# Batch 0's start shared with GpSimd and cut by head pairs, and batch 1's v behind the first pieces of w_out

## Chip, cores and metric

The kernel runs on one core of one Trainium2 chip. The metric is device time in microseconds (us), where lower is better. Engines are named as the profile names them: PE is TensorE (matmuls; PEld its weight loads), DVE is VectorE, ACT is ScalarE, POOL is GpSimd, and SP is the sync engine, which here only issues DMAs.

## What is computed

Linear attention is followed by a two-layer network with a leaky ReLU. Sizes: 8 batches, 8 heads, 576 positions, head size 64; 4608 tokens of width 512; hidden width 2048. All inputs and the output are f32 in HBM.

```python
q_s = softmax(q, axis=-1)              # over the 64 of a head
k_s = softmax(k, axis=2)               # over the 576 positions
kv  = einsum('bhsd,bhse->bhde', k_s, v)
x   = einsum('bhsd,bhde->bhse', q_s, kv) -> (4608, 512), heads side by side
h   = x @ w_in                         # 512 x 2048
out = maximum(0.01 * h, h) @ w_out     # 2048 x 512
```

## The kernel before

**Layout.** A batch of q, k or v is loaded as a tile of 128 partitions x 4 x 9 x 64: 4 "head rows" (`HL`), 9 rows of positions (`R`), and each partition half holds another head. Two head rows side by side make a head pair (`gg` is 0 or 1). After attention x is kept transposed in `xT`, four blocks of 128 channels by 4608 tokens; block `2*hh + gg` belongs to pair `gg`, so that blocks 0 and 2 come from the first pair and blocks 1 and 3 from the second. `layer1` takes the blocks in the order 0, 2, 1, 3.

**Tiles.** The network runs over 9 tiles of 512 tokens. In a tile, layer 1 makes 16 slices `j` of 128 hidden channels (4 matmuls each, then `leaky` on ACT), and layer 2 sums over the 16 slices into four 128 x 512 outputs. Tile 0 is special: its layer 1 is cut into two halves of 256 tokens, and its layer 2 runs with `j` outermost, so that the weights are needed one slice after the other. The other tiles wait for all of layer 1.

**Order.** The order of the instructions is written by hand: each engine takes its own in program order. Attention of later batches is hooked into the loops of the network: `at(t, u, ...)` files functions for tile `t` and step `u`, and `run(t, u)` calls them. In tile 0, u of 0 to 15 are the slices of the first half of layer 1, 16 to 31 those of the second half, 32 to 47 those of layer 2. Batch 1 must be done by the end of tile 0: its k and q work stands on DVE, POOL and ACT from u = 15, its kv at u = 38 (line 586), its transposes at 41 to 46, its `attend` at 47 (line 592).

**Batch 0's start (lines 507 to 557).** `q_first` (L228) takes DVE's maxima and 16 small exponentials on ACT, whose sums are collected as they run. k's maximum over the positions goes over DVE (`k_tree`, L149) and PE (`k_max_pe`, `k_all_pe`); it is subtracted from PSUM (`k_sub_ps`, L352) and ACT takes the exponential. ACT then casts v to bf16 (`v_cast`, L209), DVE normalises q's first four rows as a whole (`q_norm`, L277), PE transposes them, ACT and DVE keep the transposes, `kv_pair` (L360) and `kd_one` make the normalised kv of a pair, and `attend` (L408) makes a block of x. Layer 1 of the first 256 tokens begins with blocks 0 and 2 for j of 0 to 7 (`begun`, line 643), and takes blocks 1 and 3 afterwards. q's rows 4 and 5 (`R1`) and 6 to 8 (`R2`) follow at u = 3 and 5 and are transposed at u = 11 and 13. `wake` (L322) is a run of matmuls on zeros.

**The loads.** SP issues the plain loads (queue q1), POOL the weight loads, which cast f32 to bf16 on the way (queue q0). Both run on the same 16 DMA engines. w_in comes in two halves by hidden channels (`load_w_in`, L129), each in four pieces: two for pair 0's blocks (`gg` 0), two for pair 1's. POOL issues the first half after `gate` (line 509), a copy of one element of the second pair of batch 0's k; the second after line 534, a copy of an element that DVE's last subtraction writes. `hold_sync` (L503) makes SP wait: it issues a tiny DMA that reads the last columns of a weight piece, so whatever SP issues behind it goes out only when that piece has landed. Hold 0 (line 560) reads block 0 of w_in's second half, which its first piece brings; behind it stand batch 1's k (two pieces), q and v. POOL issues w_out in five pieces (slices 0-1, 2-3, 4-7, 8-11, 12-15; line 565) when batch 1's first k piece has landed (line 564). Hold 1 waits for w_out's fourth piece, then SP loads batch 2.

**Buffers.** PSUM has six shared banks (`psB`), taken in turn by all small products, and two for outputs.

Of the kernel before, what the change touches and what calls it, by code (L numbers as in the profile page):

```python
# [8 lines left out]
FP32 = mybir.dt.float32  # L9
BF16 = mybir.dt.bfloat16  # L10
# [9 lines left out]
L = 64  # L20
R = 9
# [4 lines left out]
def kernel(  # L26
# [122 lines left out]
    def k_tree(b, hs, steps=slice(0, 4)):  # L149
        n = hs.stop - hs.start  # L150
        ks = st[b]["k"][:, hs]
        if steps.start == 0:
            st[b]["t4"] = mx_pool.tile([P, HL, 4, D], FP32, name="t4")[:, 0:n]
        t4 = st[b]["t4"]
        t2, t1 = t4[:, :, 0:2], t4[:, :, 0]
        for o, i0, i1 in (
            (t4, ks[:, :, 0:4], ks[:, :, 4:8]),
            (t2, t2, t4[:, :, 2:4]),
            (t1, t1, t4[:, :, 1]),
            (st[b]["kmax"][:, hs], t1, ks[:, :, 8]),  # L160
        )[steps]:
            nc.vector.tensor_tensor(out=o, in0=i0, in1=i1, op=ALU.max)  # L162
# [65 lines left out]
    def q_first(b, rs):  # L228

        n = rs.stop - rs.start  # L230
        nmax = small_pool.tile([P, HL, n], FP32, name="nmax")
        qsum = small_pool.tile([P, n, HL], FP32, name="qsum")
        for hs in (slice(0, 2), slice(2, 4)):
# [3 lines left out]
            for h in range(hs.start, hs.stop):  # L237
                for r in range(n):
                    nc.scalar.activation(
                        out=st[b]["qe"][:, rs.start + r, h],  # L240
                        in_=st[b]["q"][:, h, rs.start + r],
                        func=AF.Exp,
                        bias=nmax[:, h, r : r + 1],
                        accum_out=qsum[:, r, h : h + 1],
                    )
        st[b]["qsum"] = qsum

    def q_first_rec(b, rs):
        n = rs.stop - rs.start
        st[b]["qrec", rs.start] = qrec = small_pool.tile([P, n, HL], FP32, name="qrec")  # L250
        nc.vector.reciprocal(out=qrec, in_=st[b]["qsum"])

    def q_sub(eng, b, rs):
        n = rs.stop - rs.start
# [146 lines left out]
    def q_keep(eng, b, r0, n, gs=slice(0, 4)):  # L401
        o, i = st[b]["qT"][:, gs, r0 : r0 + n], st[b]["ps", r0][:, gs]
        if eng is nc.scalar:
            eng.copy(out=o, in_=i)
        else:
            eng.tensor_copy(out=o, in_=i)
# [91 lines left out]
        st[b]["q"] = load(q, b, "q_raw", whole)  # L498
        st[b]["v"] = load(v, b, "v_raw", whole)

    held = const_pool.tile([1, 2, 128], BF16)

    def hold_sync(i, src):  # L503
        nc.sync.dma_start(out=held[:, i], in_=src)
# [45 lines left out]
    kd_rec(0, 1, 0)  # L550
    kd_rec(0, 1, 1)
    kd_one(nc.vector, 0, 1, 0)
    kd_one(nc.vector, 0, 1, 1)
    q_max(0, R1)
    q_sub(nc.gpsimd, 0, R1)
    q_max(0, R2)
    q_sub(nc.gpsimd, 0, R2)
# [12 lines left out]

    at(0, 3, lambda: q_exp(0, R1), lambda: q_sum(0, R1), lambda: q_norm(0, R1))
    at(0, 5, lambda: q_exp(0, R2), lambda: q_sum(0, R2), lambda: q_norm(0, R2))
    at(0, 11, lambda: q_transpose(0, 4, 2), lambda: q_keep(nc.vector, 0, 4, 2))
    at(0, 13, lambda: q_transpose(0, 6, 3), lambda: q_keep(nc.vector, 0, 6, 3))
    at(0, 15, lambda: attend(0, [0, 2], 256, 256, nc.scalar))
    at(0, 15, lambda: attend(0, [1, 3], 256, 256, nc.vector))
    at(0, 17, lambda: attend(0, [0, 1, 2, 3], 512, 64, nc.scalar))
    at(0, 15, lambda: k_begin(1), lambda: q_begin(1), lambda: k_tree(1, H0), lambda: k_tree(1, H1))
    at(0, 15, lambda: k_allmax(1), lambda: k_sub(nc.gpsimd, 1, H0), lambda: k_sub(nc.vector, 1, H1))
    at(0, 15, lambda: q_max(1, RA), lambda: q_sub(nc.gpsimd, 1, RA))  # L580
    at(0, 15, lambda: q_max(1, RB), lambda: q_sub(nc.gpsimd, 1, RB))
    at(0, 29, lambda: k_exp(1, H1))
    at(0, 31, lambda: k_exp(1, H0), lambda: v_cast(nc.scalar, 1, 0))
    at(0, 33, lambda: q_exp(1, RA), lambda: q_sum(1, RA), lambda: q_norm(1, RA))
    at(0, 33, lambda: v_cast(nc.scalar, 1, 1), lambda: q_exp(1, RB))
    at(0, 38, lambda: kv(1), lambda: kd_make(1), lambda: q_sum(1, RB), lambda: q_norm(1, RB))
    at(0, 41, lambda: q_transpose(1, 0, 2), lambda: q_keep(nc.scalar, 1, 0, 2))
    at(0, 42, lambda: q_transpose(1, 2, 2), lambda: q_keep(nc.scalar, 1, 2, 2))
    at(0, 45, lambda: q_transpose(1, 4, 3), lambda: q_keep(nc.scalar, 1, 4, 3))
    at(0, 46, lambda: q_transpose(1, 7, 2), lambda: q_keep(nc.scalar, 1, 7, 2))  # L590
    for i in range(8):
# [48 lines left out]
        return [g_pool.tile([P, 2, TT], BF16, name="gj") for _ in range(NF // 2)]  # L640

    g_sb = g_tiles()
    begun = []
    for j in range(0, 8, 2):
        ph = psB_pool.tile([P, 2, 256], FP32, name="ph", tag=BANK_TAG)
        for i in range(2):
            layer1(j + i, ph[:, i], 0, 256, slice(0, 2), i == 0)
        begun.append(ph)
    attend(0, [1, 3], 0, 256, nc.scalar)
    for half in range(2):  # L650
        for j in range(0, NF, 2):
            part = slice(2, 4) if begun else slice(0, 4)
            ph = begun.pop(0) if begun else psB_pool.tile([P, 2, 256], FP32, name="ph", tag=BANK_TAG)
            for i in range(2):
                layer1(j + i, ph[:, i], 256 * half, 256, part, i == 0, i == 1)
                if i == 1:
                    leaky(g_sb[j // 2][:, :, 256 * half : 256 * half + 256], ph)
                run(0, 16 * half + j + i)
# [66 lines left out]
```

## Time and profile before

| what | us |
|---|---|
| three runs | 295.09 (median), 294.68, 296.09 |
| span of the profiled execution (first to last instruction) | 293.0 |
| the profiled execution's own time | not given; the median lies 2.1 above the span |
| PE busy | 278.8 (95%) |
| ACT, DVE, POOL busy | 150.8, 144.9, 85.6 |
| PE idle before layer 1's matmuls (L452) | 4.3 |
| batch 1's attends begin on PE | 52.48 |
| granted TensorE clock, mean | 0.998 |

The timeline view has one row for a stretch of like instructions: start, duration, line, operation, tiles, shape, count, and in brackets the idle time ahead of it and what ended it. The windows view has, for each stretch, its length, the busy time of PE, PEld, DVE, ACT and POOL with the number of instructions, then the granted clock, the mean busy share of the 16 DMA engines (over 1 where transfers overlap on an engine) and the GB/s that they moved; bytes of a casting load count as bf16. The view of DMA issues gives size and time from issue to landing. A busy PE isn't a PE at its peak, since the ends of matmuls are modelled.

### The profile page before, as it was taken

The page shows a single profiled execution, that of the slowest core. Times are in us where ns is not written, and L with a number is a line of the kernel's source. Part 1 is how long each engine was busy: PE and PEld are TensorE (multiplying, and loading weights), DVE is VectorE, ACT ScalarE, POOL GpSimd, SP SyncE. Part 2 cuts the span into 40 slices and gives each one's busy share as a digit, 9 for nine tenths or more (in the row PEclk, how much of TensorE's full clock was granted, in tenths as well). Part 3 has the DMA queues.
Part 4 walks back from the last instruction along what each step waited for, and adds up shares of the span by engine and source line. Part 5 has one row for each costly group of instructions (what it writes and reads, how often), then busy time and mean ns, then how long its engine had stood idle before and what let it go on. Part 6 is the DMA issues. An engine that isn't in the chain of part 4 may idle for free.

```text
span 293.0 us, 4255 instructions
## 1 busy us (share of the span) xinstructions
PE 278.8 (95%) x1634; PEld 139.1 (47%) x1661; DVE 144.9 (49%) x240; ACT 150.8 (51%) x272; POOL 85.6 (29%) x61
## 2 busy tenths in 40 slices
PE   6596999999999999999999999999999999999995
PEld 2265845444544455454445544544455444444443
DVE  3947957885491597189367455735440200110011
ACT  4956682777058605951695338532854066007500
POOL 4645280025029307802920292029300000000000
PEclk9999999999999999999999999999999999999999
DMA  7999999694729553874399138923141310131032
GB/s 258 307 211 387 247 191 400 160 345 152 135 55 326 196 116 91 273 266 88 70 326 276 36 72 289 294 55 72 38 81 38 72 36 1 38 72 36 0 72 73
DMA packets 36580, 45.76 MB, mean 156 GB/s; under 512 B 15952, under 2 KB 19280, under 8 KB 36560
## 3 DMA queue, kind: packets, MB, share of 16 engines
q1 hardware_dynamic: 33120, 41.16, 47.4%
q0 software_dynamic: 3280, 4.20, 8.2%
q8 instruction: 13, 0.21, 0.3%
q10 hardware_dynamic: 160, 0.13, 0.1%
q14 instruction: 7, 0.06, 0.1%
HBM read 36.70 MB, written 9.44 MB: 157 GB/s over the span
## 4 chain that ended last, share of the span: by engine, by line
PE 84%; DMA 3%; DVE 3%; ACT 2%; POOL 2%; issue 1%; POOLq 0%; ACTq 0%
PE pout L473 40%; PE ph L452 39%; DMA w_in_sb<-in_moe_w_in_dram 3%; PE pkv L295 3%; PE po L440 2%; POOL k_raw L195 1%; DVE t L162 1%; ACT vb L213 1%; DVE k_raw L356 1%; ACT xT L422 1%; PE psum_qt L389 1%; POOL w_in_sb L133 0%; ACT qe L264 0%; DVE xT L424 0%; DVE m L179 0%
## 5 line engine op out<-in xcount | busy, mean ns | idle before, releaser
L452 PE MATMUL ph<-xT,w_in_sb 128*128 128x512 bf16 (+1 forms) x626 | 127.1, 357 | 4.3 <-DMA w_in_sb<-in_moe_w_in_dram 1.9
L473 PE MATMUL pout<-w_out_sb,gj 128*128 128x512 bf16 (+2 forms) x580 | 129.1, 373 | 0.9 <-issue 0.5
L461 ACT ACTIVATE gj<-ph 128x512 bf16<-128x512 f32 x144 | 82.5, 604 | 58.5 <-PE ph L452 57.9
L452 PEld LDWEIGHTS <-w_in_sb 128*128 128x128 bf16 x640 | 62.0, 98 | 66.1 <-issue 5.5
L473 PEld LDWEIGHTS <-gj 128*128 128x128 bf16 x592 | 56.9, 98 | 61.6
L467 DVE COPY out_sb<-pout 128x512 f32<-128x512 f32 (+1 forms) x34 | 22.7, 675 | 90.7 <-PE pout L473 82.1
L195 POOL TENSOR_TENSOR k_raw<-k_raw,kall 128x2304 f32<-128x2304 f32 (+1 forms) x6 | 29.1, 4844 | 86.2 <-DVE kall L187 55.8
L273 DVE TENSOR_REDUCE qsum<-qe 128x36 f32<-128x2304 bf16 (+4 forms) x11 | 19.8, 1800 | 39.5 <-ACT qe L264 39.5
L256 POOL TENSOR_TENSOR q_raw<-q_raw,qmax 128x2304 f32<-128x2304 f32 (+4 forms) x11 | 31.1, 2839 | 23.5 <-DVE qmax L226 23.5
L446 ACT CAST xT<-po 128x320 bf16<-128x320 f32 (+1 forms) x48 | 16.8, 402 | 40.0 <-PE po L440 40.0
L203 ACT ACTIVATE ke<-k_raw 128x2304 bf16<-128x2304 f32 (+2 forms) x11 | 17.5, 1595 | 9.7 <-POOL k_raw L195 9.4
L280 DVE TENSOR_TENSOR qe<-qe,qrec 128x2304 bf16<-128x2304 bf16 (+4 forms) x12 | 21.1, 1758 | 0.4
L226 DVE TENSOR_REDUCE qmax<-q_raw 128x36 f32<-128x2304 f32 (+4 forms) x11 | 19.4, 1788 | 0.0
L264 ACT ACTIVATE qe<-q_raw 128x2304 bf16<-128x2304 f32 (+4 forms) x11 | 16.9, 1535 | 0.0
L215 POOL CAST vb<-v_raw 128x1152 bf16<-128x1152 f32 x12 | 13.4, 1151 | 0.0
L467 ACT COPY out_sb<-pout 128x512 f32<-128x512 f32 (+1 forms) x3 | 1.6, 549 | 17.5 <-PE pout L473 17.5
L162 DVE TENSOR_TENSOR t<-k_raw 128x1024 f32<-128x1024 f32 (+1 forms) x10 | 10.1, 1010 | 0.4 <-DMA k_raw<-in_k_dram 0.2
L324 PE MATMUL pout<-zero 128*128 128x512 bf16 x26 | 8.9, 469 | 1.4 <-POOL zero L101 1.3
L162 DVE TENSOR_TENSOR t<-t 128x256 f32<-128x256 f32 (+2 forms) x20 | 9.6, 478 | 0.7
L440 PE MATMUL po<-qX,kd 128*128 128x320 bf16 (+1 forms) x48 | 9.8, 286 | 0.1
L295 PEld LDWEIGHTS <-ke 64*128 64x128 bf16 x252 | 7.2, 93 | 3.2 <-ACT gj L461 1.7
L295 PE MATMUL pkv<-vb,ke 64*128 64x129 bf16 x252 | 8.5, 216 | 0.1
(55 smaller groups left out, 103.5 us busy)
## 6 DMA issues: line engine op xcount, KB each, us to landing
out_dram<-out_sb SPq DMA_DIRECT2D x70, 128.0 KB, 2.4
q_raw<-in_q_dram SPq DMA_DIRECT2D x7, 1152.0 KB, 8.2
v_raw<-in_v_dram SPq DMA_DIRECT2D x7, 1152.0 KB, 11.0
k_raw<-in_k_dram SPq DMA_DIRECT2D x6, 1152.0 KB, 5.8
k_raw<-in_k_dram SPq DMA_DIRECT2D x4, 576.0 KB, 5.6
w_in_sb<-in_moe_w_in_dram POOLq DMA_DIRECT2D x8, 256.0 KB, 7.4
w_out_sb<-in_moe_w_out_dram POOLq DMA_DIRECT2D x3, 512.0 KB, 12.2
v_raw<-in_v_dram SPq DMA_DIRECT2D x2, 576.0 KB, 7.4
```

The lines of the kernel that those rows point to most:

```text
L162: nc.vector.tensor_tensor(out=o, in0=i0, in1=i1, op=ALU.max)
L195: eng.tensor_tensor(out=ks, in0=ks, in1=st[b]["kall"][:, hs].unsqueeze(2).to_broadcast([P, n, R, D]), op=ALU.subtract,)
L203: nc.scalar.activation(out=st[b]["ke"][:, :, hs].rearrange("p r h d -> p h r d"), in_=st[b]["k"][:, hs], func=AF.Exp,)
L226: nc.vector.tensor_reduce(out=m, in_=st[b]["q"][:, :, rs], axis=AX.X, op=ALU.max)
L256: eng.tensor_tensor(out=qs, in0=qs, in1=st[b]["qmax", rs.start].unsqueeze(3).to_broadcast([P, HL, n, D]), op=ALU.subtract,)
L273: nc.vector.reduce_sum(out=qsum, in_=st[b]["qe"][:, rs], axis=AX.X)
L280: nc.vector.tensor_tensor(out=qes, in0=qes, in1=st[b]["qrec", rs.start].unsqueeze(3).to_broadcast([P, n, HL, D]), op=ALU.mult,)
L295: nc.tensor.matmul(pkv[hh][:, gg, 0:129], lhsT=st[b]["ke"][rows, r, 2 * gg : 2 * gg + 2].rearrange("p h d -> p (h d)"), rhs=vb2[b % 2][row ...
L452: nc.tensor.matmul(ph, lhsT=w_in_sb[:, cb, j * P : (j + 1) * P], rhs=xT[:, cb, c0 : c0 + n], start=(i == 0 and first), stop=(i == NB - 1 a ...
L461: nc.scalar.activation(out=o, in_=ph, func=AF.Prelu, alpha=LEAKY_SLOPE)
L467: copy(out=out_sb, in_=pout)
L473: nc.tensor.matmul(pout, lhsT=g_sb[j // 2][:, j % 2, tsub * P : (tsub + 1) * P], rhs=w_out_sb[:, j, os], start=(j == 0), stop=(j == NF - 1),)
```

## The change

In batch 0, POOL opens w_in's first half on the first k pair. POOL then casts v's pairs to bf16 and multiplies q's first four rows by their reciprocal sums, a pair at a time, and issues w_in's second half behind that. PE transposes q by pairs, each pair's kv, kd and x blocks are made apart, and layer 1 is begun block by block in two groups of slices, with the other pair's attends and the transposes of rows 4 to 7 between. q's late rows go in pairs (4-5, 6-7) and row 8 alone. Two `wake` calls (4 and 3 matmuls on zeros) become one of 2. Hold 0 reads block 1 of w_in's second half, which its third piece brings. A new hold 2 on w_out's second piece stands ahead of batch 1's v. In batch 1 ACT's two casts of v stand behind the first q exponential, and hooks move.

```diff
-    R1, R2 = slice(4, 6), slice(6, R)
+    R1, R2, R3 = slice(4, 6), slice(6, 8), slice(8, R)
@@ q_first: the same work, its sums kept by pair
+    def q_first_rec(b, gg):
+        st[b]["qrec2", gg] = qrec = small_pool.tile([P, RA.stop, 2], FP32, name="qrec2")
+        nc.vector.reciprocal(out=qrec, in_=st[b]["qsum", gg])
+
+    def q_first_norm(eng, b, gg):
+        qes = st[b]["qe"][:, RA, 2 * gg : 2 * gg + 2]
+        eng.tensor_tensor(
+            out=qes,
+            in0=qes,
+            in1=st[b]["qrec2", gg].unsqueeze(3).to_broadcast([P, RA.stop, 2, D]),
+            op=ALU.mult,
+        )
+
+    def q_turn_first(b, gg):
+        n = RA.stop
+        ps = psB_pool.tile([P, 2, n, L], BF16, name="psum_q2", tag=BANK_TAG)
+        for r in range(n):
+            nc.tensor.matmul(
+                ps[:, :, r],
+                lhsT=st[b]["qe"][:, r, 2 * gg : 2 * gg + 2].rearrange("p h d -> p (h d)"),
+                rhs=ident,
+                is_transpose=True,
+                start=(r == 0),
+                stop=(r == n - 1),
+            )
+        st[b]["ps2", gg] = ps
+
+    def q_keep_first(eng, b, gg):
+        o, i = st[b]["qT"][:, gg::2, RA], st[b]["ps2", gg]
...
@@ batch 0
-    nc.gpsimd.tensor_copy(out=gate[:, 0:1], in_=st[0]["k"][:, HL - 1, R - 1, D - 1 : D])
+    nc.gpsimd.tensor_copy(out=gate[:, 0:1], in_=st[0]["k"][:, 1, R - 1, D - 1 : D])
     load_w_in(0)
...
     wake(2)
+    q_first_rec(0, 0)
+    v_cast(nc.gpsimd, 0, 0)
+    q_first_norm(nc.gpsimd, 0, 0)
     k_tree(0, H1, slice(1, 4))
...
     k_exp(0, slice(1, 2))
-    v_cast(nc.scalar, 0, 0)
-    v_cast(nc.scalar, 0, 1)
+    q_first_rec(0, 1)
+    v_cast(nc.gpsimd, 0, 1)
+    q_first_norm(nc.gpsimd, 0, 1)
+    load_w_in(1)
     k_sub_ps(0, 1)
-    nc.gpsimd.tensor_copy(out=gate[:, 0:1], in_=st[0]["k"][:, HL - 1, R - 1, D - 1 : D])
-    load_w_in(1)
+    q_turn_first(0, 0)
+    q_keep_first(nc.scalar, 0, 0)
     k_exp(0, H1)
-    q_first_rec(0, RA)
-    q_norm(0, RA)
     kv_pair(0, 0)
-    wake(4)
-    q_transpose(0, 0, 4)
-    kv_pair(0, 1)
+    wake(2)
     for hh in range(2):
         kd_rec(0, 0, hh)
         kd_one(nc.vector, 0, 0, hh)
-    q_keep(nc.scalar, 0, 0, 4, slice(0, 4, 2))
-    q_keep(nc.vector, 0, 0, 4, slice(1, 4, 2))
-    attend(0, [0, 2], 0, 256, nc.scalar)
-    wake(3)
+    attend(0, [0], 0, 256, nc.vector)
+    attend(0, [2], 0, 256, nc.scalar)
+    q_turn_first(0, 1)
+    q_keep_first(nc.vector, 0, 1)
+    kv_pair(0, 1)
...
-    hold_sync(0, w_in_sb[0:1, 0, F - 128 : F])
+    hold_sync(0, w_in_sb[0:1, 1, F - 128 : F])
     st[1]["k"] = load(k, 1, "k_raw", [(H0, ALLR), (H1, ALLR)])
     st[1]["q"] = load(q, 1, "q_raw", [(ALLH, ALLR)])
-    st[1]["v"] = load(v, 1, "v_raw", [(ALLH, ALLR)])
     nc.gpsimd.tensor_copy(out=gate[:, 0:1], in_=st[1]["k"][:, 0, 0, 0:1])
     for j0, j1 in ((0, 2), (2, 4), (4, 8), (8, 12), (12, 16)):
         load_w_out(slice(j0, j1))
+    hold_sync(2, w_out_sb[0:1, 3, 0:128])
+    st[1]["v"] = load(v, 1, "v_raw", [(ALLH, ALLR)])
     hold_sync(1, w_out_sb[0:1, 11, 0:128])
     load_all(2)
@@ hooks of tile 0: q_rest is q_exp, q_sum, q_norm
+    at(0, 0, lambda: q_rest(R1))
+    at(0, 3, lambda: q_rest(R2))
+    at(0, 12, lambda: q_rest(R3))
+    at(0, 13, lambda: attend(0, [0, 2], 256, 256, nc.scalar))
+    at(0, 13, lambda: attend(0, [1, 3], 256, 256, nc.vector))
+    at(0, 17, lambda: q_transpose(0, 8, 1), lambda: q_keep(nc.scalar, 0, 8, 1))
+    at(0, 21, lambda: attend(0, [0, 1, 2, 3], 512, 64, nc.scalar))
...
+    at(0, 31, lambda: k_exp(1, H1))
+    at(0, 33, lambda: k_exp(1, H0))
+    at(0, 36, lambda: q_exp(1, RA), lambda: q_sum(1, RA), lambda: q_norm(1, RA))
+    at(0, 36, lambda: v_cast(nc.scalar, 1, 0), lambda: v_cast(nc.scalar, 1, 1), lambda: q_exp(1, RB))
+    at(0, 36, lambda: q_sum(1, RB), lambda: q_norm(1, RB))
+    at(0, 42, lambda: kv(1), lambda: kd_make(1))
@@ layer 1 of tile 0's first 256 tokens
+    def begin(js, parts):
+        phs = [psB_pool.tile([P, 2, 256], FP32, name="ph", tag=BANK_TAG) for _ in js]
+        for i, between in parts:
+            for j, ph in zip(js, phs):
+                for h in range(2):
+                    layer1(j + h, ph[:, h], 0, 256, slice(i, i + 1), h == 0, False)
+            for fn in between:
+                fn()
+        return phs
...
+    x1 = (lambda: attend(0, [1], 0, 256, nc.scalar), lambda: attend(0, [3], 0, 256, nc.scalar))
+    t1 = (lambda: q_transpose(0, 4, 2), lambda: q_keep(nc.scalar, 0, 4, 2))
+    t2 = (lambda: q_transpose(0, 6, 2), lambda: q_keep(nc.vector, 0, 6, 2))
+    for j0, parts in ((0, ((0, x1), (1, ()))), (8, ((0, t1), (1, t2)))):
+        js = range(j0, j0 + 8, 2)
+        for j, ph in zip(js, begin(js, parts)):
+            end(j, ph, 0, slice(2, 4), False)
```

`end` gives the two blocks that are left, then `leaky` and the hooks; the second half of layer 1 runs through it as before, all four blocks at a time.

More of the change, by code (lines that the diff above doesn't have):

```diff
@@ L231, in q_first @@
         nmax = small_pool.tile([P, HL, n], FP32, name="nmax")
-        qsum = small_pool.tile([P, n, HL], FP32, name="qsum")
-        for hs in (slice(0, 2), slice(2, 4)):
+        for gg in range(2):
+            hs = slice(2 * gg, 2 * gg + 2)
+            st[b]["qsum", gg] = qsum = small_pool.tile([P, n, 2], FP32, name="qsum2")
             nc.vector.tensor_reduce(
@@ L236, in q_first @@
             )
-            for h in range(hs.start, hs.stop):
+            for h in range(2):
                 for r in range(n):
                     nc.scalar.activation(
-                        out=st[b]["qe"][:, rs.start + r, h],
-                        in_=st[b]["q"][:, h, rs.start + r],
+                        out=st[b]["qe"][:, rs.start + r, 2 * gg + h],
+                        in_=st[b]["q"][:, 2 * gg + h, rs.start + r],
                         func=AF.Exp,
-                        bias=nmax[:, h, r : r + 1],
+                        bias=nmax[:, 2 * gg + h, r : r + 1],
                         accum_out=qsum[:, r, h : h + 1],
                     )
[L246 to L251, printed above, removed]
+    def q_first_rec(b, gg):
[24 more added lines that the diff above has]
+        o, i = st[b]["qT"][:, gg::2, RA], st[b]["ps2", gg]
+        if eng is nc.scalar:
+            eng.copy(out=o, in_=i)
+        else:
+            eng.tensor_copy(out=o, in_=i)
     def q_sub(eng, b, rs):
@@ L499, in load_all @@
         st[b]["v"] = load(v, b, "v_raw", whole)
-    held = const_pool.tile([1, 2, 128], BF16)
+    held = const_pool.tile([1, 3, 128], BF16)
     def hold_sync(i, src):
@@ L575, with q_rest @@
-    at(0, 15, lambda: attend(0, [0, 2], 256, 256, nc.scalar))
-    at(0, 15, lambda: attend(0, [1, 3], 256, 256, nc.vector))
-    at(0, 17, lambda: attend(0, [0, 1, 2, 3], 512, 64, nc.scalar))
+    def q_rest(rs):
+        q_exp(0, rs)
+        q_sum(0, rs)
+        q_norm(0, rs)
+    at(0, 0, lambda: q_rest(R1))
[3 more added lines that the diff above has]
+    at(0, 13, lambda: attend(0, [1, 3], 256, 256, nc.vector))
@@ L581 @@
     at(0, 15, lambda: q_max(1, RB), lambda: q_sub(nc.gpsimd, 1, RB))
[L582 to L587, printed above, removed]
@@ L642, with end @@
     g_sb = g_tiles()
[L643 to L658, printed above, removed]
+    def begin(js, parts):
+        phs = [psB_pool.tile([P, 2, 256], FP32, name="ph", tag=BANK_TAG) for _ in js]
+        for i, between in parts:
+            for j, ph in zip(js, phs):
+                for h in range(2):
+                    layer1(j + h, ph[:, h], 0, 256, slice(i, i + 1), h == 0, False)
+            for fn in between:
+                fn()
+        return phs
+    def end(j, ph, half, part, first):
+        for h in range(2):
+            layer1(j + h, ph[:, h], 256 * half, 256, part, first and h == 0, h == 1)
+            if h == 1:
+                leaky(g_sb[j // 2][:, :, 256 * half : 256 * half + 256], ph)
+            run(0, 16 * half + j + h)
+    x1 = (lambda: attend(0, [1], 0, 256, nc.scalar), lambda: attend(0, [3], 0, 256, nc.scalar))
[5 more added lines that the diff above has]
+            end(j, ph, 0, slice(2, 4), False)
+    for j in range(0, NF, 2):
+        end(j, psB_pool.tile([P, 2, 256], FP32, name="ph", tag=BANK_TAG), 1, slice(0, 4), True)
     pout = [psO_pool.tile([P, O], FP32, name="pout") for _ in range(2)]
```

23 lines of the change are left out of this document (9 added, 14 removed).

## The prediction

> **What bounds the kernel now.** I read the page first, then the PE timeline of the first 56 us, then the DMA views, because the page's idle column points there. Times are us from the span's start.
>
> The PE timeline (start, duration, line, shape, count, idle before and its releaser):
>
> ```profile
> 17.05 1.91 PE L452 MATMUL ph<-xT,w_in_sb 128*128 128x256 bf16 x16
> ...
> 19.84 2.12 PE L452 MATMUL ph<-xT,w_in_sb 128*128 128x256 bf16 x18 [0.67 <-ACT xT L422]
> 23.89 1.69 PE L452 MATMUL ph<-xT,w_in_sb 128*128 128x256 bf16 x14 [1.92 <-DMA w_in_sb<-in_moe_w_in_dram]
> ...
> 29.04 1.03 PE L452 MATMUL ph<-xT,w_in_sb 128*128 128x256 bf16 x8 [0.72 <-ACT xT L422]
> ...
> 36.14 6.21 PE L473 MATMUL pout<-w_out_sb,gj 128*128 128x512 bf16 x27
> 42.28 1.48 PE L295 MATMUL pkv<-vb,ke 64*128 64x129 bf16 x36
> ...
> 52.48 1.96 PE L412 MATMUL po<-qT,kd 128*128 128x288 bf16 x8
> ```
>
> From 24 us PE stands still for 0.72 + 0.16, and after 54.3 in the chain for nothing over 0.05. What moves the end is when tile 1 begins, so I forecast one time: the start of batch 1's attends, 52.48 now. The idle that can go is 0.67 + 1.92 + 0.72 and whatever lies ahead of 17.05.
>
> The second row to see is what fed that 1.92. In the windows view the last two numbers are DMA share and GB/s:
>
> ```profile
> 12.00:16.00 4.00, 2.71 (x48) 1.91 (x50) 2.96 (x8) 3.87 (x5) 2.49 (x5) 1.00 1.11 201
> 22.00:23.50 1.50, 0.00 (x0) 0.00 (x0) 1.32 (x3) 1.50 (x4) 0.00 (x0) 1.00 1.01 365
> 27.50:30.00 2.50, 1.77 (x20) 1.42 (x18) 1.71 (x4) 1.07 (x2) 2.19 (x3) 1.00 1.05 405
> 30.00:32.00 2.00, 2.00 (x24) 1.80 (x23) 1.83 (x6) 1.48 (x4) 0.00 (x0) 1.00 1.13 273
> 32.00:40.50 8.50, 8.45 (x60) 5.71 (x59) 6.53 (x13) 6.29 (x9) 5.46 (x2) 1.00 1.24 209
> ```
>
> The DMA engines are full (share 1 or more) from 3 to 41 us. Plain f32 loads move at about 400 GB/s; the casting loads of the weights at 205 (counted as bf16). So 0.59 MB of k takes 1.5 us and a 0.26 MB weight piece 1.28. **The start is bound by transfers; the order of bytes is what this change can win or lose.** The SP timeline shows who opens each group:
>
> ```profile
> 19.37 0.62 SPq L504 DMA_DIRECT2D held<-w_in_sb  x1
> 20.03 1.08 SPq L79 DMA_DIRECT2D k_raw<-in_k_dram  x2
> 21.16 0.47 SPq L79 DMA_DIRECT2D q_raw<-in_q_dram  x1
> 21.67 1.39 SPq L79 DMA_DIRECT2D v_raw<-in_v_dram  x1
> 40.39 0.51 SPq L504 DMA_DIRECT2D held<-w_out_sb  x1
> ```
>
> Issue plus time to landing, one issue at a time, gives the rest: w_in's first half 14.4, 15.6, 16.9, 18.1; second half 19.4, 20.6, 21.9, 23.75; batch 1's k 25.4 and 26.9, q 29.9, v 34.4; w_out 33.8, 35.3, 37.8, 40.4, 43.1.
>
> **The parts, one by one.**
>
> *Earlier first half of w_in.* The gate opens on the first k pair (DVE starts it at 6.16) and not on the second (7.70): 1.5 us. I count 0: between 9.5 and 11.5 the view gives 365 GB/s, an f32 rate, though these pieces were issued from 7.95. They queue behind the q rest anyway. What it does give is GpSimd free at 9.0 instead of 10.5.
>
> *GpSimd takes v's casts and q's normalising.* ACT loses 2.19 (L213), DVE 1.22 + 0.25 and gains two small reciprocals of about 0.2. GpSimd gains two casts of 1.15 (L215) and two products of 512 elements. For these the nearest row is the 512-element subtraction of L256, 1.04; by the cast's rate 0.51, by L195's 3.73 for 1152 elements 1.66. I take 1.04. GpSimd: v's first half lands at 9.15, and k's max steps on DVE until 10.15 may hold it; cast to 11.2, product to 12.25, cast to 13.4, product to 14.45; then it issues w_in's second half, 1.5 later than now (12.95). The data of the first half end near 16.65 (18.1 less the 1.45 from the last byte to landing), so an issue by about 15.0 leaves no hole. Cost 0, cover 0.5 us, 1 us per us beyond it.
>
> *Head pairs and blocks.* PE has the first pair's kv at about 12.5, both x blocks near 14.8; GpSimd's second product holds pair two (kv at 14.8 to 15.5, kd to 16.5). Layer 1 starts at 15.5 to 15.8 instead of 17.05 and finishes its first 32 matmuls near 19.8. The gain is not this start but the order: at the last w_in piece 94 matmuls were open, now 80, since j 8 to 15 take the first two blocks on pieces 1 and 2 (20.6) with t1 and t2 between. Fewer wake matmuls: 0, hidden by the 0.8 us before piece 2.
>
> *Hold on piece 3 instead of piece 1.* Piece 4 then lands with no k beside it: 21.9 + 1.28 = 23.2, not 23.75. From there 80 x 0.109 = 8.7, attends 0.6, one transpose pair 0.1, a wait for the casts (0.72 now; 0 to 1.0 as R3's three DVE steps stand ahead; I take 0.3): layer 2 could start at 33.0, **3.1 us earlier**. The price is that batch 1's k is issued at 21.9 + 0.65 = 22.6, not 20.03, and the DMA engines stand empty for about 2 us.
>
> *v of batch 1 behind w_out.* An idle-queue k piece takes 3.6 from issue (the first took 4.9 with 1.3 of q ahead). So k lands at 26.2 and 27.7, q at 30.7; GpSimd issues w_out from 26.6, its data flow from 29.9: landings 32.7, 34.0, 36.5, 39.1, 41.7. Layer 2 needs them at 33.0, 34.7, 36.5, 39.9, and after kv: no stall. But v is issued behind piece 2, at 34.65, into a queue with pieces 3 to 5 in it. All remaining bytes (k and q 5.95, w_out 10.25, v 2.98 us) end at 23.8 + 19.2 = 43.0. v lands, if last, at 43.8 to 44.4; if it shares evenly from 35.8, at 42.6 to 43.2. The rows between: at 27.5 to 30 w_out got nothing beside loads issued before it, and the small hold issued at 19.37 took 4.6 to land against 2.9 at 40.39. So who comes later mostly waits; I take 44.0, 9.6 us later than now.
>
> *What then waits for v.* ACT: two casts 2.28, q_exp of rows 4 to 8 1.27. DVE: sum 1.49, reciprocal 0.28, product 1.49; kd_make waits behind these on DVE. PE: transposes 0.33, j 14 0.86, transposes 0.22, j 15 0.86. Sum 9.0, so attends start at 53.0 against 52.48. kv itself, due at 42.7 on PE, stands until 46.3. The new late thing is v; it eats the 3.1 us and 0.5 more. Break-even is a landing at 43.5.
>
> *Edits with one answer:* the hook numbers, ACT for the small keeps, the order of k's two subtractions: off that chain, 0; batch 1's k is ready by 37.1 (26.2, DVE's tree and maximum 5.95, POOL's subtraction 3.73, exp 1.17).
>
> **Sum.** +0.5 us: span 293.0 becomes 293.5. The median, 295.09, lies 2.1 above the span (the profiled run's own time isn't given), and I carry that over: **295.6**.
>
> **Rivals.**
>
> *v is served ahead of w_out's tail.* If v's bytes pass piece 5 only, v lands at 41.7, attends start at 50.7: -1.8, 293.3. For it: at 30 to 32 the view shows 273 GB/s, both kinds at once. Against it: 27.5 to 30. Chance 0.24.
>
> *Even sharing.* At 30.4 to 30.9 the two queues moved 56% and 49% of the engines' time. If that holds from arrival, v lands near 42.9: -0.6, 294.5. The Trainium skill, "DMA: Bandwidth & Descriptors", section "Queues, rings and completion order", says that each DMA engine round-robins between the queues it has work for; by that rule this rival would be the forecast. The trace agrees in that half microsecond and not at 27.5 to 30. Chance 0.10.
>
> *GpSimd is late: slower.* Place: between the first pair's cast and w_in's second half. Row: L195, 1152 elements:
>
> ```profile
> 35.05 3.73 POOL L195 TENSOR_TENSOR k_raw<-k_raw,kall 128x1152 f32<-128x1152 f32 x1 [5.36 <-DVE kall L187]
> 38.76 4.18 POOL L256 TENSOR_TENSOR q_raw<-q_raw,qmax 128x1024 f32<-128x1024 f32 x2
> ```
>
> 3.2 ns an element while DVE ran a subtraction with both inputs in SBUF for 1.36 us; 1.8 in the next row. Products of 1.66 and a cast held as long make 16 to 16.5; it decides from 15.0, and w_in, k, w_out and v all shift by 1 to 2: +2.0 in all, 297.1. The Trainium skill, "GPSIMD Engine Reference", section "Key points", says that GpSimd shares its SBUF interfaces with VectorE and contends with two-input instructions there; it speaks against moving work to GpSimd beside k's max steps, and the two rows agree. Chance 0.30.
>
> **Numbers.** Forecast 0.36 (v at 43.0 to 44.9: 294.6 to 296.5). Measurement tells about 0.5% (1.5 us) from no change. Faster 0.24 (the first rival), same 0.46 (forecast and even sharing), slower 0.30 (GpSimd late). The range leaves out the lower third of the first rival and the upper third of the last: 292.9 to 297.6.
>
> **What will show it.** GpSimd's second product should end by 15; w_in's last piece land near 23.2; the hold at 21.9 followed by a hole in the GB/s; layer 2 begin near 33; L295 stand for ACT's vb for 3 us; v land near 44 and attends start near 53. Wrong if v lands before 42, or the second half of w_in is issued after 15.5.

## The result, and the profile after

The changed kernel takes 300.22 us (median of 4 runs, 299.21 to 300.87) against 295.56 (294.68 to 296.09) for the kernel before in the same series: ratio 1.0167, 95% interval 1.0135 to 1.0199. It is slower by 4.7 us, beyond the upper end of the forecast range (297.6). The profiled execution took 299.86, 1.8 above its span of 298.1.

Batch 1's attends, the one time that the forecast hung on, begin on PE at 57.64 instead of 52.48. That is 5.16 later, and the span is 5.1 longer. So the whole loss has arisen by then.

The PE timeline of the changed kernel (start, duration, line, shape, count, idle before and its releaser); L481 is layer 1, L502 layer 2, L324 batch 1's kv, L441 the attends:

```profile
19.72 1.05 PE L481 MATMUL ph<-xT,w_in_sb 128*128 128x256 bf16 x8
...
29.79 0.38 PE L481 MATMUL ph<-xT,w_in_sb 128*128 128x256 bf16 x2 [0.69 <-ACT xT L451]
30.55 0.82 PE L481 MATMUL ph<-xT,w_in_sb 128*128 128x256 bf16 x6 [0.38 <-DVE xT L453]
...
37.55 9.66 PE L502 MATMUL pout<-w_out_sb,gj 128*128 128x512 bf16 x44
48.97 0.69 PE L324 MATMUL pkv<-vb,ke 64*128 64x129 bf16 x18 [1.77 <-ACT vb L213]
50.03 0.69 PE L324 MATMUL pkv<-vb,ke 64*128 64x129 bf16 x18 [0.37 <-ACT vb L213]
...
55.36 0.49 PE L418 MATMUL psum_qt<-ident,qe 128*128 128x128 bf16 x6 [1.50 <-DVE kd L342]
...
57.64 1.96 PE L441 MATMUL po<-qT,kd 128*128 128x288 bf16 x8
```

The stand of 1.92 for w_in is gone, as meant. In its place layer 1 starts 2.7 us later (19.72 against 17.05), and three new stands of 3.6 us in all follow v. The late start comes first, so I looked at DVE, whose max steps (L162) stand ahead of it. DVE's timeline; the first row merges two max steps:

```profile
9.26 3.87 DVE L162 TENSOR_TENSOR t<-t 128x256 f32<-128x256 f32 x2
13.17 0.29 DVE L162 TENSOR_TENSOR kmax<-t,k_raw 128x128 f32<-128x128 f32 x1
...
14.90 0.20 DVE L250 RECIPROCAL qrec<-qsum 128x8 f32<-128x8 f32 x1
```

The row of the same two steps in the kernel before:

```profile
8.81 0.74 DVE L162 TENSOR_TENSOR t<-t 128x256 f32<-128x256 f32 x2
```

They took 0.74 then and 3.87 now. No wait is shown ahead of them: the second instruction itself got longer, from 0.29 to 3.47. GpSimd's timeline in the same stretch:

```profile
9.71 1.19 POOL L215 CAST vb<-v_raw 128x1152 bf16<-128x1152 f32 x1
10.82 1.08 POOL L254 TENSOR_TENSOR qe<-qe,qrec 128x512 bf16<-128x512 bf16 x1
11.81 1.17 POOL L215 CAST vb<-v_raw 128x1152 bf16<-128x1152 f32 x1
15.18 1.04 POOL L254 TENSOR_TENSOR qe<-qe,qrec 128x512 bf16<-128x512 bf16 x1 [2.20 <-DVE qrec L250]
16.17 2.44 POOL L133 DMA_DIRECT2D w_in_sb<-in_moe_w_in_dram  x4
```

Read both together. DVE's step ends at 13.13, when GpSimd's third instruction has ended (12.98). GpSimd was not held up at all; it held DVE up, for three instructions in a row. DVE then makes the reciprocal (14.90) late, GpSimd waits 2.20 for it, and w_in's second half is issued at 16.17 instead of 12.88, as the row of before has it:

```profile
12.88 2.37 POOL L133 DMA_DIRECT2D w_in_sb<-in_moe_w_in_dram  x4
```

The windows view (length, then PE, PEld, DVE, ACT, POOL, then granted clock, DMA share and GB/s) shows what follows. The last row here is the kernel before:

```profile
14.00:16.00 2.00, 2.00 (x9) 0.74 (x9) 1.98 (x5) 1.36 (x2) 0.82 (x1) 0.50 1.12 209
16.00:18.00 2.00, 2.00 (x25) 1.22 (x22) 0.85 (x3) 1.50 (x2) 2.00 (x5) 0.50 0.70 115
...
24.00:26.00 2.00, 1.42 (x16) 1.16 (x14) 1.90 (x5) 2.00 (x5) 0.13 (x1) 1.00 0.12 23
```

```profile
14.00:16.00 2.00, 1.93 (x30) 1.29 (x30) 1.00 (x6) 1.87 (x3) 1.25 (x3) 1.00 1.12 201
```

There are two holes in the transfers, at 16 to 18 (share 0.70) from the late issue, and at 24 to 26 (0.12) from the hold. Besides, PE's granted clock stands at 0.50 here; before, it was 1.00. It fell near 11.4, some 1.2 us into the 3.25 that PE stood for DVE (10.27 to 13.51). The SP timeline closes the account:

```profile
23.78 0.63 SPq L533 DMA_DIRECT2D held<-w_in_sb  x1
24.45 1.71 SPq L79 DMA_DIRECT2D k_raw<-in_k_dram  x2
...
36.85 0.52 SPq L533 DMA_DIRECT2D held<-w_out_sb  x1
37.41 0.58 SPq L79 DMA_DIRECT2D v_raw<-in_v_dram  x1
```

v lands at 47.75. From there the chain of waits runs through ACT's two casts and an exponential, DVE's sum, reciprocal, product and kd, and PE's last transposes and slices, 9.9 us to the attends.

### The profile page after: what moved, and what is told of

It reads as the page before. It is cut to its first block, busy times and chain, and to the rows that moved or that the text cites. A ratio compares the mean times of both kernels' runs of the same rounds, so it can differ in the third digit from the quotient of the medians.

```text
span 298.1 us, 4281 instructions
## 1 busy us (share of the span) xinstructions
PE 281.6 (94%) x1656; PEld 139.3 (47%) x1656; DVE 147.7 (50%) x244; ACT 149.5 (50%) x274; POOL 90.1 (30%) x65
## 4 chain that ended last, share of the span: by engine, by line
PE 79%; DMA 11%; POOL 3%; ACT 2%; DVE 1%; issue 1%; SPq 1%; POOLq 0%
PE pout L502 38%; PE ph L481 37%; DMA v_raw<-in_v_dram 3%; DMA k_raw<-in_k_dram 3%; PE pkv L324 2%; DMA w_out_sb<-in_moe_w_out_dram 2%; DMA w_in_sb<-in_moe_w_in_dram 2%; PE po L469 2%; POOL w_in_sb L133 1%; POOL vb L215 1%; ACT vb L213 1%; POOL qe L254 1%; ACT xT L451 1%; DVE qsum L302 1%; DVE qe L309 1%
## 5 line engine op out<-in xcount | busy, mean ns | idle before, releaser
L502 PE MATMUL pout<-w_out_sb,gj 128*128 128x512 bf16 (+2 forms) x592 | 130.4, 373 | 0.0
L481 PE MATMUL ph<-xT,w_in_sb 128*128 128x512 bf16 (+1 forms) x640 | 128.2, 358 | 1.3 <-ACT xT L451 0.7
L481 PEld LDWEIGHTS <-w_in_sb 128*128 128x128 bf16 x640 | 62.1, 98 | 63.2 <-issue 2.7
L502 PEld LDWEIGHTS <-gj 128*128 128x128 bf16 x592 | 57.0, 98 | 61.7
L309 DVE TENSOR_TENSOR qe<-qe,qrec 128x2304 bf16<-128x2304 bf16 (+4 forms) x12 | 20.0, 1669 | 0.4
L215 POOL CAST vb<-v_raw 128x1152 bf16<-128x1152 f32 x14 | 15.8, 1154 | 0.0
L162 DVE TENSOR_TENSOR t<-t 128x256 f32<-128x256 f32 (+2 forms) x20 | 12.7, 635 | 0.7
L324 PE MATMUL pkv<-vb,ke 64*128 64x129 bf16 x252 | 8.5, 216 | 2.1 <-ACT vb L213 2.1
L496 ACT COPY out_sb<-pout 128x512 f32<-128x512 f32 (+1 forms) x3 | 1.7, 551 | 17.5 <-PE pout L502 17.5
L162 DVE TENSOR_TENSOR t<-k_raw 128x1024 f32<-128x1024 f32 (+1 forms) x10 | 10.1, 1011 | 0.5 <-DMA k_raw<-in_k_dram 0.2
L324 PEld LDWEIGHTS <-ke 64*128 64x128 bf16 x252 | 7.3, 93 | 5.2 <-issue 4.0
## 6 DMA issues: line engine op xcount, KB each, us to landing
w_out_sb<-in_moe_w_out_dram POOLq DMA_DIRECT2D x3, 512.0 KB, 11.4
```

Of the source, the lines that this page charges most:

```text
L309: nc.vector.tensor_tensor(out=qes, in0=qes, in1=st[b]["qrec", rs.start].unsqueeze(3).to_broadcast([P, n, HL, D]), op=ALU.mult,)
L324: nc.tensor.matmul(pkv[hh][:, gg, 0:129], lhsT=st[b]["ke"][rows, r, 2 * gg : 2 * gg + 2].rearrange("p h d -> p (h d)"), rhs=vb2[b % 2][row ...
L481: nc.tensor.matmul(ph, lhsT=w_in_sb[:, cb, j * P : (j + 1) * P], rhs=xT[:, cb, c0 : c0 + n], start=(i == 0 and first), stop=(i == NB - 1 a ...
L496: copy(out=out_sb, in_=pout)
L502: nc.tensor.matmul(pout, lhsT=g_sb[j // 2][:, j % 2, tsub * P : (tsub + 1) * P], rhs=w_out_sb[:, j, os], start=(j == 0), stop=(j == NF - 1),)
```

## The experiments

**Theory A** (the expectations of e1 to e4 call it the port theory): GpSimd's instructions in a row keep DVE's maximum of two SBUF operands from running, some 3 us; the load order (hold on piece 3, v behind w_out) costs the other 2. **Rivals**: the load order is all of it; or GpSimd slows every DVE instruction; or batch 0's work by pairs and blocks costs by itself. Each run is timed beside the kernel before on the same chip, which took 294.8 to 296.0 us (medians) in the four series.

| run | us | ratio to before, 95% | attends begin |
|---|---|---|---|
| changed kernel | 300.22 | 1.0167 (1.0135 to 1.0199) | 57.64 |
| e1_reduce | 297.33 | 1.0053 (1.0032 to 1.0075) | 55.38 |
| e2_pool_undone | 297.16 | 1.0061 (1.0039 to 1.0083) | 54.99 |
| e3_hold_piece1 | 298.21 | 1.0082 (1.0055 to 1.0109) | 55.98 |
| e4_v_early | 297.55 | 1.0073 (1.0047 to 1.0098) | 55.70 |
| e7_before_casts | 298.08 | 1.0086 (1.0053 to 1.0120) | 55.82 |
| e8_cast_last | 300.14 | 1.0160 (1.0113 to 1.0207) | 57.29 |
| e11_before_reduce | 296.79 | 1.0058 (1.0038 to 1.0079) | 54.68 |
| e6_reduce_hold1 | 295.61 | 1.0013 (0.9990 to 1.0036) | 53.32 |
| e5_reduce_loads | 293.94 | 0.9953 (0.9932 to 0.9973) | 51.72 |
| e9_no_gpsimd | 294.10 | 0.9959 (0.9943 to 0.9976) | 51.73 |
| e10_wakes | 293.08 | 0.9936 (0.9917 to 0.9955) | 50.89 |
| e12_no_gpsimd_wakes | 293.51 | 0.9932 (0.9906 to 0.9957) | 51.05 |

### e1: the second pair's maximum in one reduction, which reads one operand

```diff
+    def k_one(b, hs):
+        nc.vector.tensor_reduce(
+            out=st[b]["kmax"][:, hs],
+            in_=st[b]["k"][:, hs].rearrange("p h r d -> p h d r"),
+            axis=AX.X,
+            op=ALU.max,
+        )
-    k_tree(0, H1, slice(0, 1))
...
-    k_tree(0, H1, slice(1, 4))
+    k_one(0, H1)
```

> The changed kernel, but batch 0's second pair has its maximum over the rows taken by one DVE reduction (one input in SBUF) in place of four steps with two inputs in SBUF. GpSimd's work stays where it is. Port theory (GpSimd's casts and product hold the way that DVE's second input needs, so DVE stood from 9.7 to 13.1): DVE no longer stands, the maximum is ready near 10.5, GpSimd's second product starts near 13.0 instead of 15.2, w_in's second half is issued near 14.1 instead of 16.2, and its third piece lands near 22.0 instead of 23.8; attends start near 55.8, time about 298.4 against 300.2. Rival, order theory (the hold on piece 3 and v behind w_out make the loss, the stall is hidden behind full transfers): the stall goes and the time stays within 0.5 of 300.2. Second rival (GpSimd blocks every DVE instruction): the reduction itself takes over 3 us and nothing moves.

297.33 us, 2.9 less than the changed kernel and 1.1 less than the 298.4 that the port theory had. DVE's timeline, then GpSimd's product:

```profile
8.58 2.09 DVE L165 TENSOR_REDUCE kmax<-k_raw 128x128 f32<-128x1152 f32 x1
10.58 0.75 DVE L393 TENSOR_TENSOR k_raw<-k_raw,kallp 128x576 f32<-128x576 f32 x1
```

```profile
10.30 1.08 POOL L262 TENSOR_TENSOR qe<-qe,qrec 128x512 bf16<-128x512 bf16 x1
```

The reduction runs through GpSimd's first cast (9.19 to 10.38) and ends at 10.67. The subtraction behind it has two operands, but one of them (`kallp`) lies in PSUM; beside GpSimd's product it takes 0.75, as it did in the kernel before (9.79), where GpSimd had no such work. So not every operation with two operands is held. GpSimd's second product needs no wait, and w_in's second half is issued at 13.38. The order theory fails here (it wanted 300.2), and so does the rival that every DVE instruction is held. What is left is 2 us, and the windows view of this run shows the hole that the hold makes:

```profile
22.00:24.00 2.00, 1.67 (x18) 1.41 (x19) 1.46 (x3) 1.32 (x3) 0.00 (x0) 1.00 0.13 20
```

### e2: casts back on ACT, products on DVE

```diff
-    v_cast(nc.gpsimd, 0, 0)
-    q_first_norm(nc.gpsimd, 0, 0)
...
+    v_cast(nc.scalar, 0, 0)
+    v_cast(nc.scalar, 0, 1)
     q_first_rec(0, 1)
-    v_cast(nc.gpsimd, 0, 1)
-    q_first_norm(nc.gpsimd, 0, 1)
     load_w_in(1)
     k_sub_ps(0, 1)
+    q_first_norm(nc.vector, 0, 0)
+    q_first_norm(nc.vector, 0, 1)
```

> The changed kernel with GpSimd's part undone: v's casts on ACT, the two products on DVE, w_in's second half issued right behind the first. The rest (head pairs, blocks, hold on piece 3, v behind w_out) stays. Port theory: no stall of DVE, no late w_in; the third piece lands near 21.9, v near 45, attends near 54, time 296 to 297.5. Order theory: 299.5 or more, since the hold and v's place are untouched.

297.16 us: without GpSimd's four instructions the two max steps take 0.70 again, and the time falls by as much as with the reduction. So GpSimd's help itself, freed of its wait, gave nothing that shows here. (Two things change at once: with nothing of GpSimd's in between, w_in's second half is issued right behind the first and is out by 11.94.)

### e3 and e4: one half of the load order undone, the wait left in

```diff
@@ e3
-    hold_sync(0, w_in_sb[0:1, 1, F - 128 : F])
+    hold_sync(0, w_in_sb[0:1, 0, F - 128 : F])
@@ e4
     st[1]["q"] = load(q, 1, "q_raw", [(ALLH, ALLR)])
+    st[1]["v"] = load(v, 1, "v_raw", [(ALLH, ALLR)])
...
-    hold_sync(2, w_out_sb[0:1, 3, 0:128])
-    st[1]["v"] = load(v, 1, "v_raw", [(ALLH, ALLR)])
```

> The changed kernel with hold 0 back on w_in's first piece, so that batch 1's k is issued when piece 1 of the second half lands (near 21.2) and not when piece 3 does (23.8). Order theory: the empty stretch of the DMA engines at 24 to 26 goes, k, w_out and v all come about 2.5 earlier, time 297 or less. Port theory: the hole goes too, but w_in is still late by 2, so the gain is 1.5 to 2.5 and the time 297.7 to 298.7; w_in's fourth piece comes up to 0.5 later.

> The changed kernel with batch 1's v back in front of w_out (no hold 2). v lands near 36 instead of 47.75 and ACT's casts no longer stand; w_out comes about 2 later, its first piece near 37 to 38. Order theory: layer 2 starts later by up to 1 but kv no longer waits; attends near 55, time 297.5 or less. Port theory: the same direction, but 2 of the loss stay because w_in and k are still late: 297.5 to 298.5. If w_out's lateness takes v's place as the wait: 300 or more.

298.21 and 297.55 us. The first is where the port theory had it; the second lies on the border of both theories and decides nothing. In e3 the hole is gone (share 1.05 at 24 to 26) and v lands at 46.1. In e4 v lands at 40.5, not near 36 as I had expected, and kv stands for nothing, but layer 2 now stands 0.24 + 0.81 + 0.52 for w_out, which comes behind v. DVE's two steps take 3.89 and 3.88 in these runs. Each half is worth 2 to 2.7 us and neither brings the time of before back.

### e7 and e8: the wait in the other kernel, and at another dose

```diff
@@ e7, in the kernel before
     k_all_pe(0, 0)
     wake(2)
+    v_cast(nc.gpsimd, 0, 0)
+    v_cast(nc.gpsimd, 0, 1)
...
-    v_cast(nc.scalar, 0, 0)
-    v_cast(nc.scalar, 0, 1)
@@ e8, in the changed kernel
-    v_cast(nc.gpsimd, 0, 1)
     q_first_norm(nc.gpsimd, 0, 1)
+    v_cast(nc.gpsimd, 0, 1)
```

> The kernel before, with nothing of the change but the two v casts: moved from ScalarE to GpSimd, ahead of the second pair's max steps in the program as in the change. Theory A (GpSimd's run of instructions keeps DVE's maximum of two SBUF operands from starting until the run is over): two casts end at about 12.0, the second max step of the second pair, 0.42 us by itself, takes 2 us or more, layer 1 starts some 2 us late and the time is 296.5 to 298 us. Rival B (the wait in the changed kernel came from its new order of work, not from the engines' common way to SBUF): the max step keeps its 0.4 us and the time is 294.5 to 295.5 us, since ScalarE is 2.3 us freer.

> The changed kernel with GpSimd's last two instructions exchanged: first pair's cast, first pair's product, second pair's product, second pair's cast. The second pair's product needs a reciprocal that stands behind the max steps on DVE, so GpSimd's run ahead of it is two instructions instead of three. Theory A (the run as a whole keeps DVE out): the second pair's max step ends at 11.9 to 12.1 us instead of 13.1. Rival B (DVE gets in between two GpSimd instructions, and the third was only by chance the one it waited for): it ends at about 11.0, when the first cast is over, or still at 13.1. In both the weights' second half is issued at 15.5 to 16.5, behind the late cast, so that the time stays at 299 to 300.5 us.

e7: 298.08 us, just over the range expected. Two casts moved to GpSimd make the kernel before 3 us longer; layer 1 starts at 20.87, 3.8 later and not 2. A part of that may be the clock: in this execution it was at 0.50 from 8.3 to 18.5, beginning ahead of the casts. DVE's timeline, then GpSimd's:

```profile
9.15 1.68 DVE L162 TENSOR_TENSOR t<-t 128x256 f32<-128x256 f32 x2
10.86 2.37 DVE L162 TENSOR_TENSOR kmax<-t,k_raw 128x128 f32<-128x128 f32 x1
```

```profile
10.81 2.27 POOL L215 CAST vb<-v_raw 128x1152 bf16<-128x1152 f32 x2
```

The step that starts beside the casts takes 2.37 instead of 0.29 and ends 0.15 behind them. In the step ahead of it another 0.94 went while GpSimd was issuing w_in; in the kernel before the same issue left DVE alone (0.74 for the two steps). That part has no explanation from these runs.

e8: 300.14 us, as expected, since the late cast holds w_in's issue to 16.08. Layer 1 starts 1.2 earlier than in the changed kernel (18.55), and the time stays: so the loss goes by w_in's late issue (16.08 and 16.17) more than by layer 1's late start. The other thing that e8 tells is the dose: with two GpSimd instructions in a row (9.62 to 11.81) the two steps take 1.08 less, about one GpSimd instruction:

```profile
9.17 2.79 DVE L162 TENSOR_TENSOR t<-t 128x256 f32<-128x256 f32 x2
```

They end at 11.96, 0.15 after the second instruction, as they ended 0.15 after the third in the changed kernel and 0.15 after the second in e7. **The hold lasts as long as GpSimd's run without a pause**, and DVE doesn't get in between two of its instructions. The Trainium skill, "SBUF — State Buffer", section "SBUF: two separate sides", says that of a VectorE operation with two SBUF inputs and a GpSimd operation the first to start has the shared ports for its whole instruction and the other is blocked entirely; its section "Who interferes with whom" says that VectorE instructions with one SBUF input, outside its two-port modes, stay clear of that. e1, e7 and e8 agree in which operations get in each other's way, but the runs show a hold for several instructions and not for one. They don't settle who was first: DVE's held step is put at 9.67 in the changed kernel and at 9.58 in e8, 0.04 ahead of GpSimd's cast (9.71 and 9.62), and spans on GpSimd are rough.

### e11: is the reduction's length its own?

```diff
@@ the kernel before, with e1's reduction; GpSimd as it was
-    k_tree(0, H1, slice(0, 1))
-    k_tree(0, H1, slice(1, 4))
+    k_one(0, H1)
```

> The kernel before, with the second pair's row max in one reduction instead of four max steps, and GpSimd as it was (no cast or product there). It asks whether the reduction's 2.09 us beside GpSimd's casts is its own length. Theory A (a reduction reads one operand and runs undisturbed beside GpSimd): 2.0 to 2.1 us here too; the four steps took 1.72 us, so the time is 0 to 0.5 us over before, 295.1 to 295.6. Rival B (GpSimd slowed the reduction as well): 1.4 us here, by the 0.94 us of the maximum over 768 elements, and 294.8 to 295.1 us.

```profile
8.73 2.11 DVE L165 TENSOR_REDUCE kmax<-k_raw 128x128 f32<-128x1152 f32 x1
```

Yes: 2.11 with no GpSimd cast beside it, 2.09 with one. But my price was wrong: 296.79 us is 1.95 over the kernel before in this series, not 0 to 0.5. The second maximum came about 1 us later, PE stood 1.05 for it until 10.89, and from 11.1 on the granted clock is half (the third number from the end of the windows view, here with PE's busy time alone):

```profile
12.00:14.00 2.00, 1.41 (x6) 0.50 1.10 205
```

Layer 1's first rows follow at half speed and start at 19.73 instead of 17.05. I take this for a short delay on DVE that cost PE its clock. That the delay did it isn't shown: PE had also stood 2.21 around 7 us, against 1.69 in the kernel before.

### e5, e6 and e9: what the parts are worth without the wait

e6 is e1 with e3's hold. e5 is e1 with e3's hold, e4's place of v, and batch 1's hooks where they were. e9 is e2 with the same loads and hooks.

```diff
@@ e5 and e9: hooks of batch 1 as before
-    at(0, 31, lambda: k_exp(1, H1))
-    at(0, 33, lambda: k_exp(1, H0))
-    at(0, 36, lambda: q_exp(1, RA), lambda: q_sum(1, RA), lambda: q_norm(1, RA))
...
+    at(0, 29, lambda: k_exp(1, H1))
+    at(0, 31, lambda: k_exp(1, H0), lambda: v_cast(nc.scalar, 1, 0))
...
+    at(0, 38, lambda: kv(1), lambda: kd_make(1), lambda: q_sum(1, RB), lambda: q_norm(1, RB))
```

> The changed kernel with the second pair's row max in one reduction, and the first hold behind w_in's first piece instead of its third; w_out still ahead of v. Theory A: the hold on the third piece left the queues nearly empty for about 2 us (share 0.13 at 22 to 24 us in the run with the reduction alone), so k, q, w_out and v all come 1.5 to 2 us earlier and the time is 295.5 to 296.5 us. Rival B (the loads have no part in what is left): 297.0 to 297.6 us, as with the reduction alone.

> The changed kernel with the second pair's row max in one reduction, and with all loads and batch 1's places as before (hold behind w_in's first piece, v right behind q, the casts, sums and kv of batch 1 at the old positions). What stays of the change is batch 0's work by head pairs and blocks and GpSimd's two casts and two products. Theory A (three GpSimd instructions in a row cost about 3 us through DVE, and the load order the other 2): 294.3 to 295.8 us, no difference from before or a little less. Rival B (batch 0's work by pairs and blocks itself costs the other 2 us): 296.8 us or more, with batch 1's attends still 1.5 us or more later than the 52.5 us of before.

> The changed kernel with GpSimd's two casts back on ScalarE and its two products on VectorE, and with the loads and batch 1's places as before: what stays of the change is batch 0's work by head pairs and blocks alone, with the max steps as they were. Theory A (the pair and block order is worth the 1.2 us by which the run with reduction and old loads lies under before, and GpSimd's share in it is nothing): 293.6 to 294.6 us. Rival B (it is GpSimd's taking over that gives the gain, once its wait is out of the way): 294.9 us or more.

e6 and e9 fell where theory A had them; e5 came out 0.4 us below its range. e6, 295.61 us, is level with before. Its PE timeline still shows the price of v behind w_out, which lands at 43.44:

```profile
45.71 0.69 PE L332 MATMUL pkv<-vb,ke 64*128 64x129 bf16 x18 [0.37 <-ACT vb L221]
51.04 0.49 PE L426 MATMUL psum_qt<-ident,qe 128*128 128x128 bf16 x6 [1.50 <-DVE kd L350]
```

e5, 293.94 us, stands 0.16 for v's cast and not at all for kd, and is 0.5% faster than before. e9, 294.10, is the same without GpSimd (its w_in is also issued earlier, as in e2). So what is left of the change, the pairs and blocks with the earlier gate, is a gain of about 1 us (1.16 and 0.74 by the medians), GpSimd's part in it is nothing that can be measured, and the rival that the pair order costs falls. From the changed kernel down the steps are: the DVE wait 2.9 us (300.22 to 297.33), the hold on the third piece 1.7 (to 295.61), v behind w_out with its hooks 1.7 (to 293.94). These are medians of different series; the start of the attends gives 2.3, 2.1 and 1.6 for the same steps, so half a us of each is open.

### e10 and e12: idle matmuls in PE's stands

```diff
@@ e10: e5 with
-    wake(14)
+    wake(17)
...
     k_all_pe(0, 0)
-    wake(2)
+    wake(5)
@@ e12: e9 with
-    wake(14)
+    wake(17)
...
     k_all_pe(0, 1)
-    wake(2)
+    wake(7)
```

> The run with the reduction and the old loads, with 17 instead of 14 idle matmuls at the start and 5 instead of 2 behind the first pair's sum on TensorE. Theory A (the granted clock of 0.50 from 9 to 15 us, after TensorE stood idle around 7 and 10 us, delays batch 0's first attends and what follows): the clock stays at 1.00 there, layer 1 starts 0.5 to 1 us earlier than at 17.39 us, and the time is 293.0 to 293.6 us. Rival B (later waits take it back: layer 1's first blocks wait for copies and loads anyway): 293.7 to 294.2 us, no change.

> The run without GpSimd's casts and products and with the old loads, and with idle matmuls in TensorE's two stands: 17 instead of 14 at the start and 7 instead of 2 behind the second pair's sum, where TensorE stood 1.71 us and the granted clock then fell to 0.50 from 15 to 18 us. Theory A (the halved clock after a stand is what costs, with or without GpSimd's help): the clock stays at 1.00, layer 1 starts 0.5 to 1 us earlier than at 17.52 us, and the time is 292.9 to 293.6 us, like the run with reduction and idle matmuls (293.1) or below, since w_in's second half is issued 4 us earlier. Rival B (the clock matters only where GpSimd took over): 293.9 to 294.3 us, no change.

The same window of e5 and of e10 (length, PE busy, granted clock, DMA share, GB/s):

```profile
12.00:14.00 2.00, 2.00 (x11) 0.50 1.13 224
```

```profile
12.00:14.00 2.00, 1.76 (x28) 1.00 1.13 232
```

The clock stays at 1.00, PE gets 28 matmuls done in the stretch instead of 11 (18 of the 28 are kv's short ones), layer 1 starts at 16.11 instead of 17.39, and e10 takes 293.08 us. e12 takes 293.51: its clock is 1.00 too, its layer 1 starts at 16.83, and it isn't below e10, though its w_in was issued earlier. The two can't be told apart by their ratios. Both beat the kernel before, by 0.4 to 0.9%. That isn't the clock alone: in e10's series the executions of the kernel before with a mean clock of 0.998 or more took 294.57 to 294.84, over e10's highest (294.02). Idle matmuls in the kernel before were not tried.

## Why the prediction was wrong

**The step that failed** is in *GpSimd takes v's casts and q's normalising*: "k's max steps on DVE until 10.15 may hold it ... Cost 0". I had the two engines' conflict the wrong way round. GpSimd's durations were right (1.19, 1.08, 1.17 and 1.04 measured; 1.15 and 1.04 forecast), and I added up only GpSimd's own time. It was DVE that stood, 3.3 us in a maximum of 0.3, and the second product waits for DVE's reciprocal. The second half of w_in was issued at 16.17 instead of 14.45. e1 and e2 put the price of this step at 2.9 to 3.1 us, the longer stretch at half clock included. It is about half of the miss: with it undone, in e1, the attends still begin 2.4 us after the forecast's 53.0. The rest is in the terms on v and on what waits for v, below.

**The third rival** had the sign, the place and the deciding point (15.0), but not the cause: it made GpSimd's instructions longer, up to 1.66 a product, where they kept their length. That it named 16 to 16.5 for the issue of w_in's second half, and 16.17 came, was luck. It was priced at 2.0, and its end of the range was too near.

**Hold on piece 3.** The mechanism was right, a hole of 2 us (share 0.12, forecast "empty for about 2 us"). The times shift by GpSimd's delay: hold at 23.78 against 21.9. In e1, without that delay, it fires at 21.99 and k is issued at 22.66 (forecast 21.9 and 22.6). What it was to bring, layer 2 at 33.0, came at 34.62 there and 37.55 in the changed kernel. Of the 1.6 in e1, 0.8 is the wait for the casts (0.69 + 0.39, where 0.3 was taken); the rest isn't taken apart.

**Head pairs and blocks.** Layer 1 was to start at 15.5 to 15.8. It started at 19.72, in e5 at 17.39, in e10 at 16.11. The granted clock has no term in the prediction (the line nearest to it is "Fewer wake matmuls: 0"), and that was a second miss: it was 0.50 from 11.4 to 18.3, and in e5, without the DVE wait, still from 9.0 to 15.8. The wake matmuls that the change took out are not shown to be the reason, since the one call that is left in their place stands at 17.5 and at 15.6, after the clock had fallen. e10, with other idle matmuls added, prices the clock at 0.9 us by the medians and 0.8 by the attends; the intervals of the ratios of e5 and e10 overlap.

**v of batch 1 behind w_out.** It was to be issued at 34.65 and to land at 44.0, 9.35 later; e1 has 35.03 and 45.49, e6 32.97 and 43.44, the changed kernel 37.41 and 47.75: 10.3 to 10.5 after the issue in each. The DMA view shows what lies between: in the changed kernel v has no bytes for some 3.5 us after its issue, and from 42 to 44 the two queues share about evenly (59% and 54% of the engines' time). So the late comer waits and then shares, and the forecast was 1 us too short. Both rivals that served v sooner fell by their times.

**What waits for v** was to take 9.0 us and took 9.9: I had left out DVE's kd (0.7), for which PE's transposes now wait 1.50, as they take the PSUM bank that kv held. e6 tests the break-even: v at 43.44, just where I had put it, gave attends at 53.32, 0.84 late.

**The sum.** On the forecast's 53.0, v is 3.75 later and the chain behind it 0.9 longer: 57.6, as measured. Of the 3.75, 1.9 are at the hold, 0.9 are added until v is issued, and 1.0 between issue and landing.

## What to carry to other kernels

When work is moved to GpSimd, look at what DVE does at the same time: price the move by DVE's instructions with two operands in SBUF that will start beside GpSimd's, and count GpSimd's whole run without a pause, not one instruction. Give DVE a form with one SBUF operand there, if it isn't dearer than the wait (in e11, where nothing held DVE, the reduction was a loss), or put the work elsewhere. And where a change makes PE stand a microsecond longer early on, look at the granted clock in that window before taking the delay for its own length.

## What the runs showed of the hardware that I had not expected

- DVE's hold lasted for two or three GpSimd instructions in a row, to 0.15 us after the last (2.79 and 3.87 us for steps that take 0.74).
- The granted clock fell to 0.50 after stands well under 3 us, and the length of one stand doesn't decide it. In e5 it fell at 9.0, behind a stand of 1.75. e9 kept 1.00 behind one of 1.80 in the same place and fell at 15.3, 1.7 us after one of 1.71. e1 fell at 13.0 with no stand over 1.14 since its first matmul. The kernel before, in its profiled execution, kept 1.00 through stands of 1.69 and 1.44. The Trainium skill, "TensorE: Matmul & The Clock Gate", section "HAM oscillation — how this bites in real kernels", warns of idle gaps beyond about 3.4 us; the changed kernel stood for 3.25, but its clock fell some 1.2 us into that, and e1, e5 and e9 lost the clock with stands of about half the rule's or less. What decides stays open.
- The clock differs between executions of one kernel. Over the 17 executions of the kernel before in e10's series its mean was 0.987 to 1.000. Nine executions of e9 with a mean of 0.993 or 0.994 took 293.95 to 294.25, the tenth, at 1.000, took 293.28. With the idle matmuls of e10 and e12 the mean was 0.998 or more in every execution.
- A load issued while another queue was full (v in the six runs that have it behind w_out's first pieces: the changed kernel, e1, e2, e3, e6 and e8) took 10.3 to 10.6 us from issue to landing whatever the time of its issue, against 9.35 estimated from the bytes ahead of it.
